# A reordered plan for windowed attention with a gated feed-forward: GpSimd's instructions beside VectorE's on PSUM

## The chip, the cores and the metric

The kernel runs on one core of one Trainium2 chip. The metric is device time in microseconds of one execution. TensorE (PE in the profile) multiplies matrices and writes to PSUM; VectorE (DVE), ScalarE (ACT) and GpSimd (POOL) do elementwise work; SyncE (SP) issues all transfers here. Each engine works through its own instructions in the order in which the program issues them, and waits at one whose inputs or output buffer are not ready.

## The reference

```python
batch, n_heads, seq, head_dim = (8, 8, 576, 64)
scores = scale * np.matmul(q, k.transpose(0, 1, 3, 2))
mask = (rel >= 0) & (rel < window)            # window = 64
scores = np.where(mask, scores, -1000000000.0)
scores = scores - np.max(scores, axis=-1, keepdims=True)
attn = np.exp(scores)
attn = attn / (np.sum(attn, axis=-1, keepdims=True) + 1e-09)
attn_out = np.matmul(attn, v)
...
x = attn_out.transpose(0, 2, 1, 3).reshape(B * S, H * D)     # 4608 tokens x 512
h = x @ w_in                                   # 512 x 2048
sp = np.maximum(h, 0.0) + np.log1p(np.exp(-np.abs(h)))
g = h * erf(sp)
return (g @ w_out).astype(np.float32)          # 2048 x 512
```

## The kernel before

The 4608 tokens are cut into 36 units of 128 tokens for the attention and 18 chunks of 256 tokens (two units) for the feed-forward. A chunk's feed-forward is done in two groups, one for each half of the 2048 hidden columns, so there are 36 groups `g`. Products are built from float16 pairs: each operand is split into a high part (a scaled copy, `scaled` or `narrow`) and a low part (what is left, `rest`), and three products are added.

The order of the whole program is written out by hand in one string, `PLAN`, of 2794 tokens. A token names a function and its arguments; where it ends in `v`, `a` or `g`, that letter puts the instruction on VectorE, ScalarE or GpSimd. The program issues the tokens one after the other, so the string fixes the order on every engine and in SP's queue of transfers. The steps are, with their tokens and lines:

- Loads of a unit: `lq`, `lk`, `lv` (L376 to L382). `pk` takes the largest magnitude of each (L392 on ScalarE, L394 on VectorE); `pa pb px py pc` turn the maxima into a chunk's scales.
- `qh kh vh` make the high parts (L366 ScalarE, L368 VectorE, L370 GpSimd) and `ql kl vl` the low parts (L373, VectorE).
- `s` is the score product (L449), `m` adds the mask and takes the row maximum from PSUM (L458, VectorE), `f` subtracts it (L463), `e` takes the exponential twice on ScalarE (L472, L473), `r` makes the low part (L477), `t` transposes by DMA (L480), `a` multiplies by the values (L487), `n` divides by the sum from PSUM (L492 to L494).
- `xh`, `xl` split the output (L504 or L502, L510) and `xt` transposes it by DMA. From group 8 on, the first feed-forward product is a seven-product (Strassen-like) one: `T` makes sums of `x` (L520, three steps with the index k), `yh` and `yl` split them (L504 or L502, L531; part 0 has 768 columns and part 1 has 512), `yt` transposes them.
- `M:g:m` is one of the seven products (L705). Products 1, 6, 7 and 4 pile up in one PSUM bank, and after each of them `E:g:k` copies the bank out (L502 on ScalarE, L504 on VectorE). Products 2, 5 and 3 pile up in the other, and `C:g:k` adds the bank to `h` (L720, VectorE). The next product into a bank waits for that reader. The first groups use `mm` and `ev` instead (L661).
- `sp` and `er` are softplus and erf on ScalarE (L726, L730), `gt` multiplies by `h` (L734, VectorE), `gh` and `gl` split the gated values (L366 or L368, L373), `mA` and `mB` are the second product with the high and with the low part (L753), `fo` scales or adds it into the output (L762, L368 or L366), `st` stores.
- `dc` and `gn` are one instruction each on a few scale columns (L646, L651).
- The weights are loaded by `L` and split at the start (`d c o b mb mx my mc h l dg lp le`); `U Uh Ul` make the weight sums of the seven products (L689, L502 or L504, L695).

ScalarE has one table of functions active at a time. Exponential, softplus and erf stand in different tables, and each change costs an `ACT_TABLE_LOAD`; the order of `e`, `sp` and `er` on ScalarE sets how many there are.

From about group 23 on the string repeats with a period of one chunk: two groups of feed-forward and two units of attention. The attention runs some chunks ahead of the feed-forward, so the last four groups have no attention beside them.

Of the kernel before, what the change touches and what calls it, by code (L numbers as in the profile page):

```python
# [19 lines left out]
W = 64  # L20
# [30 lines left out]
    "lq:0 lk:0 s:0 lm lq:1 m:0:1 f:0:1:g lk:1 lv:0 m:0:0 pk:0:2:v lv:1 e:0:1 f:0:0:g s:1 e:0:0 m:1:0 L:1 pk:1:2:v "  # L51
    "pa:0 r:0:1:g pb:0 f:1:0:v px:0 L:0 r:0:0:v L:3 py:0 pc:0 t:0:0 c:1 vh:1:a d:1 lq:2 c:0 m:1:1 o:1 lk:2 d:0 "
    "f:1:1:v o:0 vh:0:g s:2 d:3 t:0:1 e:1:0 c:3 b:0:a vl:0 a:0:0 b:1:a o:3 a:0:1 vl:1 L:2 mb:0 L:9 r:1:0:v d:2 e:1:1 "
    "c:2 L:8 lq:3 o:2 b:3:a mx:0 t:1:0 b:2:a m:2:0 my:0 c:9 mc:0 r:1:1:g m:2:1 L:11 dg:0 h:0:v d:9 n:0 f:2:0:g "
    "f:2:1:g lv:2 h:1:a c:8 lp:0:1 lp:1:0 t:1:1 o:9 lv:3 lk:3 xh:0:a mb:1 le:0:1:a d:8 lk:4 le:1:0:a d:11 lq:4 "
    "lp:0:0 pk:2:2:v mx:1 L:10 c:11 pk:3:2:v lp:1:1 s:3 my:1 o:8 e:2:0 xl:0:g L:4 e:2:1 a:1:0 L:5 a:1:1 b:9:a b:8:a "
    "o:11 m:3:0 pa:1 c:10 le:0:0:a pb:1 xt:0:0 mc:1 r:2:0:g n:1 xt:0:1 r:2:1:g m:3:1 h:2:a xh:1:a le:1:1:a px:1 mb:4 "
    "t:2:0 f:3:0:g pk:4:0:v dg:1 t:2:1 f:3:1:g py:1 lp:2:0 mx:4 pc:1 xl:1:v d:10 o:10 lp:2:1 vh:2:a my:4 dc:0:g vl:2 "
    "h:3:v b:11:a vh:3:v b:10:a a:2:0 a:2:1 e:3:1 lk:5 xt:1:1 mb:5 e:3:0 le:2:1:a xt:1:0 le:2:0:a mm:0:0 vl:3 "
    "ev:0:0:a mx:5 pk:4:1:a mc:4 my:5 lv:4 r:3:0:g l:3 dg:4 pk:4:2:v mc:5 lq:5 dg:5 n:2 c:4 L:6 xh:2:v t:3:0 h:9:a "  # L60
    "pk:5:1:a mm:0:1 h:10:v r:3:1:g d:4 mm:0:2 lv:5 o:4 h:11:a t:3:1 pk:5:0:a pk:5:2:v c:5 L:7 lp:9:1 ev:0:1:a a:3:1 "
    "pa:2 a:3:0 xl:2:g pb:2 xt:2:0 n:3 px:2 ev:0:2:v xh:3:a le:9:1:v lp:9:0 mm:0:3 b:4:a c:7 py:2 ev:0:3:a xt:2:1 "
# [12 lines left out]
    "t:4:1 h:12:g L:15 a:4:0 fo:1:1:a a:4:1 er:2:0 n:4 xh:4:v pk:9:1:a W:1 vh:6:a lp:12:1 ql:7 dc:6:g t:5:1 lp:12:0 "
    "d:15 t:5:0 mm:2:2 f:6:0:g a:5:1 vl:6 dc:7:v L:14 dc:4:v f:6:1:g c:15 ev:2:2:a le:12:1:a c:14 o:15 a:5:0 n:5 "
    "d:14 o:14 le:12:0:a mm:2:3 b:15:a mm:3:0 b:14:a lq:9 mb:7 vh:7:g s:7 vl:7 xh:5:a mx:7 my:7 xl:4:g ev:2:3:a "
    "ev:3:0:v mm:3:1 e:6:1 pk:9:0:a e:6:0 xl:5:v lv:9 xt:5:0 gt:2:0 lv:8 mc:7 V:1 m:7:0 h:15:v r:6:1:v dg:7 ev:3:1:v "
    "mm:3:2 xt:5:1 pk:8:2:v pk:9:2:v gh:2:0:a lp:15:0 lp:15:1 r:6:0:g le:15:0:v pa:4 sp:3:0 gl:2:0 mm:3:3 h:14:g "
    "xt:4:1 sp:2:1 m:7:1 f:7:0:g le:15:1:a pb:4 px:4 er:2:1 t:6:0 xt:4:0 mA:2:0:1 ev:3:2:a t:6:1 U:0:7:0:0:v er:3:0 "  # L80
    "py:4 a:6:1 a:6:0 l:14 f:7:1:v ev:3:3:a mA:2:0:0 U:0:7:1:0:v pc:4 gt:3:0 U:0:7:2:0:v sp:3:1 gt:2:1 gn:3:g mm:4:0 "
    "Uh:0:7:0:a mB:2:0:0 gh:2:1:a e:7:0 gh:3:0:a Ul:0:7:0:v kh:8:v kl:8 U:1:7:0:0:v gl:2:1 gn:2:g lk:10 vh:8:v "
    "mB:2:0:1 r:7:0:v ev:4:0:a e:7:1 mA:2:1:0 er:3:1 mm:4:1 U:1:7:1:0:g gl:3:0 kh:9:g t:7:0 mA:2:1:1 n:6 U:1:7:2:0:v "
    "ev:4:1:a r:7:1:v Uh:1:7:0:a mm:4:2 kl:9 t:7:1 qh:8:a gt:3:1 ql:8 Ul:1:7:0:v U:2:7:0:0:g xh:6:a mB:2:1:1 "
    "mB:2:1:0 s:8 a:7:0 fo:2:1:v a:7:1 m:8:1 sp:4:0 fo:2:0:v lk:11 lq:10 gn:5:v m:8:0 st:0:1 U:2:7:1:0:g mm:4:3 "
    "gh:3:1:a vh:9:a f:8:1:v n:7 mA:3:0:0 vl:9 gl:3:1 lv:11 mB:3:0:0 mA:3:1:0 er:4:0 xl:6:g qh:9:a ev:4:3:v gt:4:0 "
# [745 lines left out]
```

## Time and profile before

| what | value |
|---|---|
| median of three runs | 913.55 us (910.85 to 913.95) |
| profiled execution | 915.73 us, of which the span of instructions is 914.0 us |
| TensorE busy | 843.7 us, 92% |
| VectorE busy | 776.8 us, 85%, 1644 instructions |
| ScalarE busy | 696.7 us, 76% |
| GpSimd busy | 279.6 us, 31%, 230 instructions |
| granted TensorE clock, mean | 0.983 |

A line of a group names the source line, the engine, the operation, output and inputs by the program's names, shapes and count; then the busy time in us, the mean of one in ns, and the idle time of the engine just before these instructions with what ended it. A line of the timeline has the start in us, the duration in us, the engine, the line and the operation, and in square brackets the idle time before it with its releaser. A line of a stretch has its bounds, its length, and then the busy us of PE, weight loads (PEld), DVE, ACT and POOL with instruction counts, the granted clock, the busy share of the DMA engines and the GB/s that they moved.

### The profile page before, as it was taken

To read this page: it belongs to the slowest core of one execution; us is meant where nothing else is said; L and a number is where in the kernel's file an instruction comes from. 1 tells how busy PE (TensorE), PEld (TensorE's weight loads), DVE (VectorE), ACT (ScalarE), POOL (GpSimd) and SP (SyncE) were. 2 spreads that over 40 slices of the span, in tenths; PEclk is the share of its full clock that TensorE was granted. 3 is DMA by queue.
4 is the path that set the end of the run, shared out by engine and by line. 5 is a ranking of instruction groups with operands and counts; after the bars stand their busy time and mean duration, and the time that the engine had idled before them with its cause. 6 is when DMAs were issued, how large, how long until landed. Compare 5 with 4: busy or idle time off the path is not lost.

```text
span 914.0 us, 25226 instructions
## 1 busy us (share of the span) xinstructions
PE 843.7 (92%) x10726; PEld 583.9 (64%) x10726; DVE 776.8 (85%) x1644; ACT 696.7 (76%) x848; POOL 279.6 (31%) x230
## 2 busy tenths in 40 slices
PE   2579999998998999999998899999999999999998
PEld 2256556666676677667667567676767676766763
DVE  6789999999997998999796999999999997655453
ACT  5779889987997899877886678777777876644551
POOL 2431532422262564323234323232323232200000
PEclk9789999999998999999999999999999999999999
DMA  9992474364374744565363545455444432311000
GB/s 336 367 269 79 157 193 97 89 132 105 74 166 50 188 97 119 124 114 129 88 111 73 128 96 126 90 125 91 115 102 115 102 68 45 74 39 21 24 15 33
DMA packets 163489, 104.34 MB, mean 114 GB/s; under 512 B 140208, under 2 KB 140336, under 8 KB 163376
## 3 DMA queue, kind: packets, MB, share of 16 engines
q1 hardware_dynamic: 163376, 102.73, 47.0%
q8 instruction: 84, 1.38, 0.6%
q14 instruction: 29, 0.24, 0.1%
HBM read 59.44 MB, written 9.44 MB: 75 GB/s over the span
## 4 chain that ended last, share of the span: by engine, by line
DVE 38%; PE 36%; ACT 13%; issue 6%; DMA 5%; SPq 1%; POOL 1%; DVEq 0%; ACTq 0%; POOLq 0%
PE o L753 16%; PE hp L705 15%; DVE gl L373 5%; DVE sm L458 4%; DVE y L734 3%; DVE vs L373 2%; DVE h L720 2%; PE hp L661 2%; ACT y L726 2%; DVE qs L373 2%; DVE arena L531 2%; DVE gh L368 2%; ACT y L730 2%; ACT L730 2%; DVE peaks L394 2%
## 5 line engine op out<-in xcount | busy, mean ns | idle before, releaser
L753 PE MATMUL o<-w,gh 128*128 128x512 f16 x1152 | 269.2, 381 | 1.9 <-DVE ob L762 1.2
L753 PEld LDWEIGHTS <-gh 128*128 128x128 f16 x1152 | 109.2, 98 | 121.7 <-issue 5.9
L705 PE MATMUL hp<-arena,w 128*128 128x128 f16 x2688 | 168.9, 221 | 11.6 <-DVE h L504 10.1
L705 PEld LDWEIGHTS <-w 128*128 128x128 f16 x2688 | 158.9, 99 | 28.9 <-issue 14.5
L502 ACT ACTIVATE h<-hp 128x512 f32<-128x512 f32 x112 | 65.9, 589 | 113.3 <-PE hp L705 105.4
L753 PE MATMUL o<-w,gl 128*128 128x512 f16 x576 | 142.5, 379 | 1.3 <-DVE gl L373 1.1
L705 PEld LDWEIGHTS <-arena 128*128 128x128 f16 x2016 | 118.1, 98 | 18.3 <-issue 5.6
L705 PE MATMUL hp<-arena 128*128 128x128 f16 x2016 | 125.3, 220 | 4.6 <-ACT h L502 4.6
L373 DVE SCALAR_TENSOR_TENSOR gl<-y,sgh,gh 128x1024 f16<-128x1024 f32 x72 | 101.5, 1419 | 18.5 <-ACT gh L366 12.0
L734 DVE TENSOR_TENSOR y<-h,y 128x1024 f32<-128x1024 f32 x72 | 92.0, 1282 | 13.5 <-ACT y L730 13.5
L463 POOL TENSOR_TENSOR sm<-sm,mx 128x512 f32<-128x512 f32 x45 | 60.8, 1353 | 104.0 <-DVE mx L458 92.2
L661 PE MATMUL hp<-arena,w 128*128 128x256 f16 x768 | 87.6, 273 | 3.4 <-ACT h L502 2.0
L753 PEld LDWEIGHTS <-gl 128*128 128x128 f16 x576 | 52.5, 98 | 55.1 <-DVE gl L373 2.5
L720 DVE TENSOR_TENSOR h<-hp,h 128x512 f32<-128x512 f32 x84 | 57.3, 683 | 35.2 <-PE hp L705 35.2
L661 PEld LDWEIGHTS <-w 128*128 128x128 f16 x768 | 74.6, 98 | 17.5 <-issue 4.8
L726 ACT ACTIVATE y<-h,c 128x1024 f32<-128x1024 f32 x72 | 80.1, 1143 | 2.2 <-DVE gl L373 1.6
L477 POOL TENSOR_TENSOR p<-sm,p 128x512 f16<-128x512 f32 x33 | 44.8, 1357 | 119.8 <-ACT sm L473 117.1
L730 ACT ACTIVATE y<-y 128x1024 f32<-128x1024 f32 x72 | 75.3, 1053 | 0.5
L458 DVE CUSTOM_DVE_ANT_0 sm<-s,mask 128x128 f32<-128x128 f32 x288 | 65.3, 281 | 7.6 <-PE s L449 7.5
L366 ACT ACTIVATE gh<-y,sgh 128x1024 f16<-128x1024 f32 x45 | 51.3, 1140 | 23.0 <-DVE y L734 15.4
L726 ACT ACT_TABLE_LOAD x41 | 52.6, 1283 | 18.3 <-DVE h L720 17.6
L730 ACT ACT_TABLE_LOAD x46 | 59.0, 1283 | 0.8
(163 smaller groups left out, 1274.8 us busy)
## 6 DMA issues: line engine op xcount, KB each, us to landing
vr<-v_in SPq DMA_DIRECT2D x36, 512.0 KB, 4.1
kr<-k_in SPq DMA_DIRECT2D x36, 384.0 KB, 3.9
qr<-q_in SPq DMA_DIRECT2D x36, 256.0 KB, 3.9
out<-ob SPq DMA_DIRECT2D x34, 256.0 KB, 2.5
arena<-w_in SPq DMA_DIRECT2D x4, 1024.0 KB, 10.1
w<-w_in SPq DMA_DIRECT2D x4, 1024.0 KB, 7.0
arena<-w_out SPq DMA_DIRECT2D x4, 1024.0 KB, 5.5
w<-w_out SPq DMA_DIRECT2D x4, 512.0 KB, 9.2
```

The lines of the kernel that those rows point to most:

```text
L366: nc.scalar.activation(dst, src, AF.Copy, scale=s)
L373: nc.vector.scalar_tensor_tensor(dst, src, s, hi, op0=ALU.mult, op1=ALU.subtract)
L458: nc.vector.tensor_tensor_reduce(smi(u, par)[:, j, :], sps[par][:, j, :], mask[:, var, :], 1.0, LOWEST, op0=ALU.add, op1=ALU.max, accum_ou ...
L463: eng_of(eng).tensor_tensor(s, s, m.unsqueeze(2).broadcast_to([P, HP, P]), op=ALU.subtract)
L502: nc.scalar.activation(dst, src, AF.Copy)
L661: nc.tensor.matmul(hps[pc % 2][:, f, :], w1[a][:, cc, fs], xt[b][c % 2][:, cc:2 * NCC:NCC, :], start=(n == 0), stop=(n == 3 * NCC - 1))
L705: nc.tensor.matmul(bank[:, q, f, :], left(m, a, 2 * hf + q)[:, cc, f * P:(f + 1) * P], xt[b][c % 2][:, slot + cc, :], start=m in (1, 2, 5) ...
L720: nc.vector.tensor_tensor(dst, bank_view(1), dst, op=ALU.add)
L726: nc.scalar.activation(at(yb, g, n), at(hb, g, n), AF.Softplus, scale=st_c[g][:, n:n + 1])
L730: nc.scalar.activation(y, y, AF.Erf)
L734: nc.vector.tensor_tensor(y, at(hb, g, n), y, op=ALU.mult)
L753: nc.tensor.matmul(ops[j], a[:, f, ts], w2[b][:, hf * GF + f, :], start=f == 0 and a is gh and b == 0, stop=f == GF - 1 and a is gl)
```

## The change

Only `PLAN` changes. The same 2794 steps are issued in another order, and some with another engine letter. Counted over the whole string, these numbers of instructions change engines (net):

| step | VectorE | ScalarE | GpSimd |
|---|---|---|---|
| `yl` (768 columns / 512 columns) | -7 / -8 | | +7 / +8 |
| `vh` | +7 | | -7 |
| `T`, steps 0 / 1 / 2 | +7 / -3 / +6 | | -7 / +3 / -6 |
| `r` | +5 | | -5 |
| `kh` | | +6 | -6 |
| `E` | +5 | -5 | |
| `fo` | +4 | -4 | |
| `xh` | +4 | -4 | |
| `h` | -6 | +3 | +3 |
| `U`, `f`, `qh` | +3, +1, +2 | 0, 0, -1 | -3, -1, -1 |
| `gh` | -2 | +2 | |
| `dc` | -10 | | +10 |
| `gn` | -4 | | +4 |
| `pk` of q / of k | -6 / +6 | +6 / -6 | |

The order of ScalarE's steps gives 38 softplus, 44 erf and 32 exponential table changes, against 41, 46 and 38 before. The string again repeats with a period of one chunk in its second half. GpSimd has ten instructions in such a chunk, against eleven: before `T` (steps 2 and 0), `gn`, `f` three times, `kh`, `r` twice, `xl` and `vh`; after `T` (step 1), `f` twice, `xl`, `yl` twice, `r`, `dc` and `gn` twice.

At the start, the loads of the first weights and of the values come ahead of the first keys and queries. The diff, cut to the start and to one repeated chunk (from `M:26:1` on):

```diff
-    "lq:0 lk:0 s:0 lm lq:1 m:0:1 f:0:1:g lk:1 lv:0 m:0:0 pk:0:2:v lv:1 e:0:1 f:0:0:g s:1 e:0:0 m:1:0 L:1 pk:1:2:v "
...
-    "lv:33 r:30:0:g xt:28:1 mA:23:1:0 gl:24:0 t:30:0 gl:23:1 M:26:1 pk:32:1:a t:30:1 mB:23:1:1 E:26:0:a pk:33:0:v "
-    "C:25:2 M:26:6 pk:33:2:v yh:14:0:v E:26:1:a T:14:1:v s:31 pa:16 pb:16 fo:23:1:v T:14:2:g mB:23:1:0 gn:29:g px:16 "
-    "gh:24:1:v py:16 sp:25:0 M:26:2 pc:16 fo:23:0:v sp:25:1 qh:32:v mA:24:0:1 qh:33:a m:31:0 kh:32:v kl:32 M:26:7 "
-    "er:25:1 mA:24:0:0 C:26:0 f:31:0:g E:26:2:a gt:25:1 er:25:0 ql:32 M:26:5 kh:33:g m:31:1 M:26:4 ql:33 E:26:3:a "
-    "dc:28:v a:30:1 gl:24:1 a:30:0 s:32 n:30 f:31:1:g mB:24:0:0 gt:25:0 e:31:1 mB:24:0:1 M:27:1 C:26:1 kl:33 "
-    "gh:25:0:a vh:32:a M:26:3 yt:14:0:0 mA:24:1:1 C:26:2 e:31:0 gn:24:v r:31:1:v dc:33:v mA:24:1:0 E:27:0:v t:31:0 "
-    "r:31:0:g yh:14:1:v sp:26:0 st:11:1 m:32:1 M:27:6 lk:35 t:31:1 sp:26:1 vl:32 mB:24:1:1 st:11:0 yl:14:1:v M:27:2 "
-    "m:32:0 f:32:1:g er:26:0 mB:24:1:0 C:27:0 E:27:1:a yl:14:0:v a:31:1 xh:30:a a:31:0 lq:34 gl:25:0 yt:14:0:1 "
-    "M:27:7 e:32:1 lv:34 gh:25:1:v yt:14:1:1 M:27:5 E:27:2:v xl:30:g fo:24:1:v M:27:4 vh:33:g xt:30:0 fo:24:0:a "
-    "f:32:0:v mA:25:0:1 gt:26:0 E:27:3:a mA:25:0:0 r:32:1:v pk:34:0:a n:31 lk:34 pk:35:1:a er:26:1 mB:25:0:0 C:27:1 "
-    "T:15:0:g lq:35 mB:25:0:1 e:32:0 vl:33 pk:34:2:v mA:25:1:1 gt:26:1 gh:26:0:a yt:14:1:0 M:27:3 lv:35 r:32:0:g "
-    "xt:30:1 mA:25:1:0 gl:26:0 t:32:0 gl:25:1 M:28:1 pk:34:1:a t:32:1 mB:25:1:1 E:28:0:a pk:35:0:v C:27:2 M:28:6 "
...
+    "L:0 d:0 lv:1 pk:1:2:v c:0 o:0 lv:0 L:1 pk:0:2:v lk:0 pa:0 c:1 lq:0 pb:0 px:0 d:1 s:0 b:0:a lm o:1 lq:1 py:0 "
...
+    "pk:32:0:a t:30:0 M:26:1 r:30:1:v m:31:0 yt:13:0:1 lv:33 mA:23:1:0 E:26:0:a n:29 sp:25:0 M:26:6 T:14:0:v "
+    "mB:23:1:0 pk:33:2:v E:26:1:v T:14:1:g mA:23:1:1 pk:32:2:v C:26:0 pa:16 fo:23:0:v yh:14:0:v M:26:7 gh:24:0:v "
+    "yt:14:0:0 gl:24:0 mB:23:1:1 E:26:2:a st:11:0 pb:16 t:30:1 fo:23:1:v M:26:5 m:31:1 er:25:0 M:26:4 px:16 er:25:1 "
+    "C:26:1 f:31:1:g py:16 xl:28:g M:26:3 gt:25:1 mA:24:0:1 pc:16 gt:25:0 mA:24:0:0 qh:32:a E:26:3:a ql:32 f:31:0:v "
+    "M:27:1 gh:24:1:v e:31:1 mB:24:0:0 kh:32:v kl:32 mB:24:0:1 qh:33:a T:14:2:v gh:25:0:a C:26:2 xt:28:1 a:30:0 "
+    "gl:24:1 a:30:1 e:31:0 s:32 M:27:2 ql:33 E:27:0:a r:31:0:v M:27:6 kh:33:v r:31:1:v sp:26:1 dc:31:v t:31:1 "
+    "yh:14:1:v mA:24:1:1 C:27:0 yl:14:1:g sp:26:0 lk:34 st:11:1 E:27:1:a yt:14:1:1 kl:33 mA:24:1:0 vh:32:v gl:25:0 "
+    "er:26:0 t:31:0 mB:24:1:0 gh:25:1:a M:27:7 fo:24:0:v xt:28:0 m:32:0 mB:24:1:1 m:32:1 f:32:0:g mA:25:0:0 lq:35 "
+    "vl:32 e:32:0 mB:25:0:0 dc:32:g f:32:1:v yt:14:1:0 E:27:2:v gn:31:g M:27:5 e:32:1 r:32:0:g lq:34 M:27:4 gn:26:g "
+    "n:30 yl:14:0:g lk:35 lv:34 C:27:1 pk:34:1:v a:31:0 er:26:1 a:31:1 s:33 vh:33:v fo:24:1:a xh:30:a gl:25:1 M:27:3 "
+    "E:27:3:a mA:25:0:1 C:27:2 gt:26:0 mB:25:0:1 vl:33 pk:35:1:a M:28:2 sp:27:1 gt:26:1 pk:35:0:a pk:34:0:a t:32:0 "
...
```

377 rows, old and new, of the table PLAN are left out of this document.

## The prediction, on record before the result

> **What bounds the kernel now.** I read the page first, then the busy time by stretches: the start, the aperiodic middle, the repeated chunks, and one such chunk.
>
> ```profile
> span 914.0 us, 25226 instructions
> PE 843.7 (92%) x10726; PEld 583.9 (64%) x10726; DVE 776.8 (85%) x1644; ACT 696.7 (76%) x848; POOL 279.6 (31%) x230
> 0.00:75.00 75.00, 42.77 (x469) 27.01 (x470) 58.82 (x161) 53.27 (x77) 27.43 (x37) 0.86 1.01 308
> 75.00:477.00 402.00, 384.64 (x4912) 266.51 (x4911) 375.34 (x833) 351.62 (x441) 148.81 (x113) 0.99 0.51 117
> 477.00:753.00 276.00, 260.45 (x3717) 186.92 (x3716) 254.01 (x526) 212.10 (x248) 90.91 (x70) 0.99 0.47 103
> 660.95:706.97 46.02, 43.93 (x626) 31.36 (x626) 43.03 (x90) 35.82 (x42) 14.39 (x11) 1.00 0.47 110
> ```
>
> PE is busy for 843.7 of 914.0 us, so 70.3 us is all that any order can win: 32.2 in the first 75 us (DMA share 1.01), 17.4 in the middle, 15.6 in the repeated chunks, some 5 behind them. A chunk takes 46.02 us; PE is busy for 43.93 of it and DVE for 43.03. Both are nearly full, so I ask who waits for whom in that chunk, and look at the place in the timeline just ahead of 660.95.
>
> ```profile
> DVE gl L373 <- ACT gh L366: 2.0, 1, 2.0
> PE hp L705 <- DVE h L504: 1.7, 1, 1.7
> ...
> 656.31 1.37 POOL L510 TENSOR_TENSOR arena<-arena 128x512 f16<-128x512 f32 x1 [2.50 <-ACT arena L502]
> 656.59 2.18 DVE L373 SCALAR_TENSOR_TENSOR gl<-y,sgh,gh 128x1024 f16<-128x1024 f32 x1
> 657.67 2.09 POOL L370 TENSOR_SCALAR vs<-vr,csc 128x1024 f16<-128x1024 f32 x1
> 658.69 1.61 DVE L368 TENSOR_SCALAR gh<-y,sgh 128x1024 f16<-128x1024 f32 x1
> 660.22 0.67 DVE L504 COPY h<-hp 128x512 f32<-128x512 f32 x1
> 660.95 1.22 PE L705 MATMUL hp<-arena,w 128*128 128x128 f16 x19 [1.68 <-DVE h L504]
> ```
>
> Of PE's 2.09 idle us, 1.68 is one wait: the next product waits for the copy `E` (L504), and ahead of that copy stand `gl` with 2.18 us and `gh` with 1.61, both beside POOL. What these cost without POOL is seen at the end of the run (from 822 us on, POOL idle):
>
> ```profile
> L373 DVE SCALAR_TENSOR_TENSOR gl<-y,sgh,gh 128x1024 f16<-128x1024 f32 x10 | 12.6, 1278 | 6.0 <-PE o L753 4.9 <-ACT gh L366 1.1
> L720 DVE TENSOR_TENSOR h<-hp,h 128x512 f32<-128x512 f32 x10 | 6.9, 688 | 18.4 <-PE hp L705 18.4
> L368 DVE TENSOR_SCALAR gh<-y,sgh 128x1024 f16<-128x1024 f32 x5 | 3.7, 745 | 0.0
> L504 DVE CAST arena<-arena 128x512 f16<-128x512 f32 x1 | 0.4, 417 | 0.0
> ```
>
> So POOL lengthens `gl` by 0.90 us and `gh` by 0.87 there, together 1.77: the 1.68 us of PE. Reading PSUM costs DVE nothing: `C` (L720) takes 688 ns alone and 683 over the whole run.
>
> ```profile
> L720 DVE TENSOR_TENSOR h<-hp,h 128x512 f32<-128x512 f32 x84 | 57.3, 683 | 35.2 <-PE hp L705 35.2
> ```
>
> The Trainium skill, "SBUF — State Buffer", section "Who interferes with whom", gives the rule: GpSimd and VectorE share one port pair as a lock; a VectorE instruction with two SBUF inputs or in a two-port mode collides, one with at most one SBUF input outside those modes does not. The trace agrees as to who collides. By a full lock `gl` would lose what was left of the POOL instruction, 1.09 us, where the trace gives 0.90; with 1.09 the sum below would gain about 0.2 us a chunk, 1 us in all.
>
> **The change, part by part.** The rows of the one chunk on DVE:
>
> ```profile
> L373 DVE SCALAR_TENSOR_TENSOR gl<-y,sgh,gh 128x1024 f16<-128x1024 f32 x4 | 5.9, 1504 | 2.0 <-ACT gh L366 2.0
> L734 DVE TENSOR_TENSOR y<-h,y 128x1024 f32<-128x1024 f32 x4 | 5.0, 1239 | 0.0
> L458 DVE CUSTOM_DVE_ANT_0 sm<-s,mask 128x128 f32<-128x128 f32 x16 | 3.6, 279 | 0.0
> L373 DVE SCALAR_TENSOR_TENSOR vs<-vr,csc,vs 128x1024 f16<-128x1024 f32 x2 | 3.2, 1598 | 0.0
> L373 DVE SCALAR_TENSOR_TENSOR ks<-kr,csc,ks 128x768 f16<-128x768 f32 x2 | 2.7, 1342 | 0.0
> L368 DVE TENSOR_SCALAR gh<-y,sgh 128x1024 f16<-128x1024 f32 x2 | 2.3, 1174 | 0.0
> L531 DVE TENSOR_TENSOR arena<-arena 128x512 f16<-128x512 f32 x1 | 1.5, 1525 | 0.0
> L762 DVE SCALAR_TENSOR_TENSOR ob<-o,sg,ob 128x512 f32<-128x512 f32 x2 | 1.5, 738 | 0.0
> L477 DVE TENSOR_TENSOR p<-sm,p 128x512 f16<-128x512 f32 x2 | 1.4, 680 | 0.0
> L394 DVE TENSOR_REDUCE peaks<-vr 128x1 f32<-128x512 f32 x2 | 1.3, 674 | 0.0
> L646 DVE TENSOR_SCALAR c<-kw,cpw 128x2 f32<-128x2 f32 x2 | 1.2, 610 | 0.0
> L504 DVE CAST arena<-arena 128x512 f16<-128x512 f32 x1 | 1.0, 976 | 0.0
> L531 DVE TENSOR_TENSOR arena<-arena 128x768 f16<-128x768 f32 x1 | 0.9, 941 | 0.0
> L368 DVE TENSOR_SCALAR ks<-kr,csc 128x768 f16<-128x768 f32 x1 | 0.6, 615 | 0.0
> L504 DVE CAST arena<-arena 128x768 f16<-128x768 f32 x1 | 0.6, 552 | 0.0
> ...
> 692.12 1.01 DVE L373 SCALAR_TENSOR_TENSOR ks<-kr,csc,ks 128x768 f16<-128x768 f32 x1
> 804.42 1.34 PE hp L705 x24
> 805.76 1.73 PE o L753 x8
> ```
>
> *Contention in a repeated chunk.* Above the lone price: `gl` 4 x 0.226 = 0.90, `vl` 2 x 0.32 = 0.64 (same form as `gl`), `kl` 2 x 0.33 = 0.66 (against 1.01 at 692.12), `gh` 2 x 0.43 = 0.86, `yl` 0.845 (against the 680 ns of the same shape), the cast 0.56: 4.5 us of DVE.
>
> *Work moved in that chunk.* DVE gains `T` step 0 (0.68), one `r` (0.68), one `f` (0.68, same shape), one `kh` (0.615) and two `vh` (0.745 each, the form of `gh`): 4.1. It loses both `yl` (0.94 and, alone, 0.68), one `dc` (0.61) and one `qh` (some 0.5, by its size against `kh`): 2.7. One `gn` less and `pk` of k for q cancel within 0.3 (estimate). Net +1.4.
>
> *Contention that stays.* `f:31:1` follows `m` and runs beside `px` and `C:26:1`, `f:32:0` beside `m:32:1`, `r` beside `n`, `T` step 1 beside `pk`: none of these DVE instructions reads two SBUF tensors at length. But `xl:28` comes straight behind `f:31:1`, when DVE is at `gt:25:1`: up to 1.37 (its price at 656.31); I take 1.1, since `f` overlaps a little less than planned. `yl:14:1` outlasts `C:27:0` by 1.37 - 0.68 and meets `kl:33`: 0.6. `yl:14:0` has half as many columns again, about 2.1 (estimate); `C:27:1` and `pk:34:1` cover most: 0.3. The small `dc` and `gn` and the ends of `f`: 0.4. Sum 2.4; bounds 0 and the 4.5 of now or somewhat above. DVE's chunk comes to 43.0 - 4.5 + 1.4 + 2.4 = 42.3 us, 0.7 below now: not much, so it is the place that decides.
>
> *PE's wait.* Ahead of `E:26:1` on DVE there now stand `m`, `n`, `T` and `pk` in place of `gl` and `gh`, and PE has `mB` before product 6: the 1.68 us go. What is late next is `C:26:1`, for which product 3 waits. From the end of product 6 DVE has to do `E` 0.67, `pk` 0.67, `C` 0.68, `pa` 0.3 (estimate), `fo` 0.74, `yh` 0.55, `gh` 0.75, `gl` 1.28, `fo` 0.74, `m` 1.0 (four of 0.28, overlapped), `px` 0.4 (estimate), `C` 0.68: 8.5 us. PE in that time has two `mB` (0.87 each, half of the 1.73), one `mA` 1.73, three products of 1.34 and about 0.4 of `pb` and `py`: 7.9. That leaves a wait of 0.6. Elsewhere PE has slack: `M:27:2` comes some 2 us behind `C:26:2`. So a chunk wins 1.7 - 0.6 = 1.1, and the 276 us of repeated chunks, six of them, 6.5 us. Bounds: 12.5 won (all 2.09 each) and, where DVE keeps all contention, the loss under the rivals.
>
> *The middle.* Unrepeated order, DVE 375 of 402 us busy, POOL 17.0 us per 46 against 14.4 in the chunk: the same disease, but 17.4 us of idle PE are all that can go. I take 7; bounds 0 and 12. A step that serves both `E` and `fo` moves from ScalarE to DVE here (five and four instructions, 0.67 and 0.74 each): hidden only while DVE has room, which the removed contention gives.
>
> *Table loads.* Eleven fewer (114 against 125) at the price of this row, 14.1 us of ACT:
>
> ```profile
> L726 ACT ACT_TABLE_LOAD x41 | 52.6, 1283 | 18.3 <-DVE h L720 17.6
> 4.63 1.99 PE L449 MATMUL s<-kr,qr 64*64 64x128 f32 x32 [4.63 <-DMA kr<-k_in]
> ```
>
> ACT is busy for 35.8 of 46 us in a chunk, so most is covered by PE's and DVE's work: I count 1 us in the middle; bounds 0 and 3. Nine more splits on ACT (`kh` +6, `h` +3) use up most of what the loads free.
>
> *The start.* Two pieces of `w_in` and two units of values now go through SP's queue ahead of the first keys: by their shapes 3.1 MB, at the 308 GB/s of this stretch 10 us, and the first scores wait for keys (4.63 us now). The bytes needed before the first feed-forward product are nearly the same, and the weights' own chain starts earlier. I take +2; bounds -4 and +10.
>
> *SP and POOL as queues.* In a chunk `t:30:1` now stands behind `yt:14:0:0` and a store, and `t:31:0` behind `yt:14:1:1`, which waits for POOL's `yl:14:1`; `a:31` is a dozen PE steps later, so I cost it at nothing. If that cover went, `a` would wait for the rest of a POOL instruction, 1 to 2 us a chunk. The end without attention: 0.
>
> Sum: +2 - 7 - 6.5 - 1 = -12.5, so 903.2 against the profiled 915.73. The median of the runs is 2.2 below that execution, so 901.
>
> **The rivals.**
>
> *The waits only move (915).* The place ahead of `C:26:1` is 0.6 by my count, with 8.5 against 7.9; if `T`, `r` and `vh` make DVE late before product 6 too, the chunk gives the 1.7 back. For it: DVE has only 3.0 idle us a chunk and gets 1.4 of work. Against: 4.5 of contention.
>
> *DVE becomes the bound (slower, 927).* POOL's instructions start when their inputs come, not when DVE reads PSUM. If they still meet `gt`, `kl` and `gl`, DVE has 43.0 + 1.4 and its 3.0 of waits: 47.4, or +1.4 a chunk, +20 over the 678 us with attention; with half of that in the middle, +13. It decides once more than 4.5 - 1.4 = 3.1 us of contention stay. The same page of the Trainium skill says that whoever starts first holds the pair for the whole instruction; by that, a late POOL start ahead of `gt` costs all of it. For it: `xl` and `yl` have no PSUM work long enough beside them.
>
> *All of PE's waits go (886).* Chunks -12.5, middle -12, start -2, tables -1: 915.73 - 27.5, less 2.2. For it: nearly all slack in PE's new order is over 1 us. Against: the middle also waits for DMAs and tables.
>
> **How the numbers follow.** Forecast 0.50 (892 to 909), all waits gone 0.17, only moved 0.15, DVE bound 0.18. About 0.5% is what a measurement of this kernel tells from no change: 909 to 918. Faster 0.67, same 0.15, slower 0.18. The range reaches into both outer cases: 884 to 922; the likeliest case's own is 892 to 909.
>
> **What would show it.** `gh` (L368) near 750 ns and `gl` (L373) below 1400; `E`'s 1.7 us wait gone from a chunk, with a shorter one of `C` (L720); a chunk of 44.5 to 45.2 us; POOL's chunk below 14.39. Wrong: a chunk of 46 or more, `gt` (L734) well above 1239, or a first feed-forward product more than 5 us later.

## The result and the profile after

The changed kernel takes 890.89 us (median of four runs, 889.11 to 891.25) against 912.2 us (910.39 to 913.95): a ratio of 0.9763 with a 95% interval of 0.9735 to 0.979, 21.3 us faster. The forecast was 901 in a range of 884 to 922. The time lies in the range, 1 us below the likeliest case's own 892 to 909 and nearer to the rival of 886 than to 901. The direction was right; the gain is 21.3 us where 12.5 was forecast. The profiled execution took 891.25 us, its span 889.5.

From the page of after: the span, the engines, and the chain that ended last by engine.

```profile
span 889.5 us, 25238 instructions
PE 839.4 (94%) x10726; PEld 581.8 (65%) x10726; DVE 750.6 (84%) x1647; ACT 689.3 (77%) x840; POOL 248.1 (28%) x229
...
PE 62%; DVE 19%; DMA 7%; ACT 5%; issue 3%; POOL 2%; SPq 1%; DVEq 0%; POOLq 0%; ACTq 0%
```

The same chain of before:

```profile
DVE 38%; PE 36%; ACT 13%; issue 6%; DMA 5%; SPq 1%; POOL 1%; DVEq 0%; ACTq 0%; POOLq 0%
```

Read the chain first: before, the last instruction goes back through VectorE and ScalarE for half of the span, after through TensorE for 62% of it. The busy time by the same stretches as before, and one repeated chunk (columns as in the prediction):

```profile
0.00:75.00 75.00, 39.41 (x434) 23.43 (x434) 50.27 (x146) 49.57 (x69) 23.05 (x33) 0.89 1.00 292
75.00:477.00 402.00, 395.71 (x4999) 273.98 (x5000) 378.46 (x857) 360.08 (x454) 142.61 (x122) 0.99 0.54 124
477.00:753.00 276.00, 272.59 (x3981) 198.65 (x3979) 253.97 (x562) 214.27 (x249) 72.71 (x64) 1.00 0.50 102
663.62:708.08 44.46, 43.63 (x626) 31.33 (x626) 41.66 (x91) 36.24 (x43) 11.87 (x11) 1.00 0.53 111
```

Length less PE's busy time is PE's idle time. It went from 32.2 to 35.6 us in the first 75 us, from 17.4 to 6.3 in the middle, from 15.6 to 3.4 in the repeated chunks, and from 5.2 to 4.8 behind them: 20.2 us less in all. PE's busy time fell by another 4.3 (843.7 to 839.4). Together that is the 24.5 us between the spans.

The groups of VectorE that the prediction named, over the whole run:

```profile
L373 DVE SCALAR_TENSOR_TENSOR gl<-y,sgh,gh 128x1024 f16<-128x1024 f32 x72 | 93.4, 1299 | 4.4 <-ACT gh L366 2.7 <-PE o L753 1.2
L734 DVE TENSOR_TENSOR y<-h,y 128x1024 f32<-128x1024 f32 x72 | 89.5, 1254 | 4.2 <-ACT y L730 4.2
L368 DVE TENSOR_SCALAR gh<-y,sgh 128x1024 f16<-128x1024 f32 x25 | 20.4, 815 | 2.1 <-PE o L753 2.1
```

`gl` takes 1299 ns (1419 before, 1278 alone) and `gt` 1254 (1282 before); `gh` takes 815 (1021 before) where 745 is the price alone. A collision here is a VectorE instruction lengthened by a GpSimd instruction beside it. Summed over VectorE's instructions with a GpSimd one beside them, each by its time above the median of those of its line, tiles and form that have none, the collisions cost VectorE some 74 us before and 36 after (73.8 and 35.8, worked out from the two traces). What that bought in one chunk, from the waits of after in 663.62 to 708.08 (us in all, times, longest):

```profile
PE hp L705 <- DVE h L720: 0.4, 1, 0.4
...
PE av L412 <- DVE cdiag L409: 0.4, 1, 0.4
```

The 1.7 us wait for the copy `E` (L504) is gone. A wait of 0.44 for `C` (L720) is what came next, and the timeline of after shows where it is from:

```profile
661.92 1.04 POOL L463 TENSOR_TENSOR sm<-sm,mx 128x512 f32<-128x512 f32 x1 [7.48 <-DVE mx L458]
662.00 0.97 DVE L409 SCALAR_TENSOR_TENSOR cdiag<-ctop,ident 3x3 bf16<-3x3 f32 x1
662.90 0.67 DVE L720 TENSOR_TENSOR h<-hp,h 128x512 f32<-128x512 f32 x1
662.91 2.81 POOL L510 TENSOR_TENSOR arena<-arena 128x512 f16<-128x512 f32 x1
...
663.50 1.20 DVE L734 TENSOR_TENSOR y<-h,y 128x1024 f32<-128x1024 f32 x1
663.62 1.50 PE L705 MATMUL hp<-arena,w 128*128 128x128 f16 x24 [0.44 <-DVE h L720]
...
664.81 0.94 DVE L361 TENSOR_SCALAR csc<-cpw 128x3 int32<-128x3 int32 x1
...
675.69 1.16 POOL L531 TENSOR_TENSOR arena<-arena 128x512 f16<-128x512 f32 x1 [9.97 <-issue]
676.08 1.59 DVE L373 SCALAR_TENSOR_TENSOR ks<-kr,csc,ks 128x768 f16<-128x768 f32 x1
```

Directly ahead of `C` on VectorE stands `cdiag`, three by three elements, part of `px`: 0.97 us, because `f` runs on GpSimd beside it. That is the collision that is left on PE's path.

### The profile page after: what moved, and what is told of

Same layout as the page of the kernel before. It is cut to its first block, busy times and chain, and to the rows that moved or that the text cites. A ratio compares the mean times of both kernels' runs of the same rounds, so it can differ in the third digit from the quotient of the medians.

```text
span 889.5 us, 25238 instructions
## 1 busy us (share of the span) xinstructions
PE 839.4 (94%) x10726; PEld 581.8 (65%) x10726; DVE 750.6 (84%) x1647; ACT 689.3 (77%) x840; POOL 248.1 (28%) x229
## 4 chain that ended last, share of the span: by engine, by line
PE 62%; DVE 19%; DMA 7%; ACT 5%; issue 3%; POOL 2%; SPq 1%; DVEq 0%; POOLq 0%; ACTq 0%
PE o L753 30%; PE hp L705 22%; PE hp L661 3%; PE av L487 2%; PE s L449 2%; DVE gl L373 2%; DVE sm L458 2%; DMA pt<-p 2%; PE o L624 2%; DMA pt<-arena 1%; DMA arena<-w_out 1%; DVE y L734 1%; DMA kr<-k_in 1%; DMA qr<-q_in 1%; DVE misc L689 1%
## 5 line engine op out<-in xcount | busy, mean ns | idle before, releaser
L753 PE MATMUL o<-w,gh 128*128 128x512 f16 x1152 | 268.8, 379 | 2.0 <-DVE ob L762 0.9
L753 PEld LDWEIGHTS <-gh 128*128 128x128 f16 x1152 | 109.0, 98 | 119.7 <-issue 2.8
L705 PE MATMUL hp<-arena,w 128*128 128x128 f16 x2688 | 164.6, 219 | 3.2 <-DVE h L720 1.7
L705 PEld LDWEIGHTS <-w 128*128 128x128 f16 x2688 | 155.2, 98 | 17.1 <-issue 4.9
L753 PE MATMUL o<-w,gl 128*128 128x512 f16 x576 | 144.6, 379 | 0.0
L502 ACT ACTIVATE h<-hp 128x512 f32<-128x512 f32 x108 | 63.1, 587 | 71.2 <-PE hp L705 69.1
L373 DVE SCALAR_TENSOR_TENSOR gl<-y,sgh,gh 128x1024 f16<-128x1024 f32 x72 | 93.4, 1299 | 4.4 <-ACT gh L366 2.7
L734 DVE TENSOR_TENSOR y<-h,y 128x1024 f32<-128x1024 f32 x72 | 89.5, 1254 | 4.2 <-ACT y L730 4.2
L463 POOL TENSOR_TENSOR sm<-sm,mx 128x512 f32<-128x512 f32 x44 | 52.3, 1194 | 138.2 <-DVE mx L458 117.2
L753 PEld LDWEIGHTS <-gl 128*128 128x128 f16 x576 | 54.0, 98 | 55.3
L661 PEld LDWEIGHTS <-w 128*128 128x128 f16 x768 | 75.5, 99 | 15.6 <-issue 3.0
L720 DVE TENSOR_TENSOR h<-hp,h 128x512 f32<-128x512 f32 x84 | 57.5, 684 | 31.3 <-PE hp L705 28.7
L366 ACT ACTIVATE gh<-y,sgh 128x1024 f16<-128x1024 f32 x47 | 53.6, 1141 | 27.5 <-PE o L753 23.4
L473 ACT ACTIVATE sm<-sm,shift,cde 128x512 f32<-128x512 f32 x64 | 52.1, 814 | 2.1
```

Source lines behind the costliest of these rows:

```text
L366: nc.scalar.activation(dst, src, AF.Copy, scale=s)
L373: nc.vector.scalar_tensor_tensor(dst, src, s, hi, op0=ALU.mult, op1=ALU.subtract)
L463: eng_of(eng).tensor_tensor(s, s, m.unsqueeze(2).broadcast_to([P, HP, P]), op=ALU.subtract)
L502: nc.scalar.activation(dst, src, AF.Copy)
L661: nc.tensor.matmul(hps[pc % 2][:, f, :], w1[a][:, cc, fs], xt[b][c % 2][:, cc:2 * NCC:NCC, :], start=(n == 0), stop=(n == 3 * NCC - 1))
L705: nc.tensor.matmul(bank[:, q, f, :], left(m, a, 2 * hf + q)[:, cc, f * P:(f + 1) * P], xt[b][c % 2][:, slot + cc, :], start=m in (1, 2, 5) ...
```

## The experiments

The theory to test: VectorE's instructions that read two SBUF tensors or copy within SBUF were lengthened by GpSimd's, where PE waited for what stood behind them, and the change moved those instructions apart. The rivals: the order itself, ScalarE's tables, or work taken off an engine. Ratios are to the kernel before, run on the same chip. Kernels with added tokens have their lines a little lower: `T` at L522 and `gl` at L375, for instance. The end of a chunk is that of its last second product (L753) in the profiled execution.

**The order without the letters, and the letters without the order.**

```diff
 e1: the changed kernel's order; each step on the engine that it had before
-T:14:1:g  yl:14:1:g  vh:33:v ...
+T:14:1:v  yl:14:1:v  vh:33:g ...
 e2: the order of before; each step on the engine that it has after
```

> The changed order with every step on the engine it had before; the letters alone are undone. Theory A (the gain is that GpSimd's instructions stand where VectorE does not need the shared port, which takes order and letters together): the letters no longer fit their places, so the contention per repeated chunk is back near the 4.5 to 6 us of before and the time is 903 to 918. Theory B (the gain is the new order on TensorE, with more work between a product and the reader of its bank, and fewer table loads): the order keeps it, 890 to 898. TensorE's waits tell: by A the waits of L705 for VectorE's copies stand near the 9 us of before in the repeated stretch, by B under 3.

> The order of before with the engine letters of the changed kernel. Theory A: the 15 yl on GpSimd and the rest are not placed for this order, contention stays at 4 us a chunk or more, 908 to 922. Theory B: no new order, no gain, 910 to 925. A third theory, C (the gain is simply less GpSimd work, 248 against 280 us busy): most of the gain, 893 to 902.

Measured: 951.16 us for e1 (ratio 1.0436, 1.0414 to 1.0458) and 943.75 for e2 (1.0361, 1.0332 to 1.039). Nothing forecast that: each half alone loses more than the whole gains. Stretches of e1 (first), and of e2 (middle and a repeated chunk):

```profile
75.00:477.00 402.00, 358.99 (x4324) 245.42 (x4323) 347.38 (x764) 317.40 (x406) 135.50 (x101) 0.95 0.45 106
```

```profile
75.00:477.00 402.00, 357.58 (x4418) 246.24 (x4417) 354.89 (x769) 329.24 (x410) 139.15 (x108) 0.96 0.46 109
666.80:711.10 44.30, 43.76 (x626) 31.24 (x627) 41.71 (x90) 35.23 (x43) 13.52 (x10) 1.00 0.51 112
```

The loss is in the unrepeated middle: PE is busy for 359 and 358 of 402 us there, against 385 before and 396 after. In the repeated chunk the letters alone do what the whole change does, 44.3 us against 46.0, and the order alone does two thirds of it: 45.0 in e1 (718.7 to 763.7), with 5.5 us of collisions still in VectorE's chunk against 5.9 before, but a wait for `E` of 0.8 in place of 1.7. So the sum of the collisions does not decide there. Whether e1 gains by collisions at other places or by more work of PE ahead of the reader, which was theory B, is not separated. The repeated part is a question of its own. In the middle, order and letters seem to be a matched pair: DVE, ACT and PE are all less busy in e1 and e2, so they wait for each other. That is read from the busy times, and no run here tests it further.

**Two steps moved, nothing else.** The kernel before, with `xl` and `vh` of the repeated chunks on VectorE, so that POOL has nothing beside `gl` and `gh` ahead of `E`:

```diff
-xl:30:g  vh:33:g
+xl:30:v  vh:33:v
```

> The kernel before, with only ten steps of the last five chunks with attention changed: xl of units 26 to 34 and vh of units 27 to 35 go from GpSimd to VectorE, in their places (both behind the copy E:2 in VectorE's order). These are the two GpSimd instructions beside which gl took 2.18 us and gh 1.61. Theory A: gl and gh there fall to 1.28 and 0.75, TensorE's 1.68 us wait for E:2 goes, and a chunk falls from 46.0 to 44.3 to 45.3 us although VectorE does 1.4 us more work; about 4 chunks, so 907 to 911. Rival (VectorE's sum of work decides): the 1.4 us more are a longer chunk, 46.0 to 47.4, and 912 to 918.

Measured: 903.55 us (0.991, 0.9889 to 0.9932), 8.5 us below before, more than expected. Two repeated chunks of it, and PE's waits in 580 to 670:

```profile
580.60:625.00 44.40, 43.99 (x628) 31.40 (x627) 42.68 (x92) 35.88 (x43) 11.08 (x9) 1.00 0.55 111
625.00:669.30 44.30, 43.89 (x627) 31.29 (x627) 42.58 (x92) 35.78 (x43) 11.08 (x9) 1.00 0.51 113
```

```profile
PE av L404 <- DVE cmx L358: 0.5, 2, 0.2
PE hp L705 <- DVE h L720: 0.3, 2, 0.2
```

VectorE was given two more instructions a chunk (90 to 92) and is busy for less (43.03 to 42.6), and the wait for `E` is gone with 1.6 to 1.7 us of the chunk. That shows the mechanism: the collision, not the amount of work, held PE. It also gives as much in a repeated chunk as the whole change. The plan of e3 is that of before up to the end of chunk 9, and yet the profiled execution of before ends that chunk at 540.1 us and that of e3 at 535.5. So a difference of some 4 us between single executions says nothing in the middle; the medians and the repeated chunks do.

The same in the middle as well, from unit 8 on:

> The kernel before, with the local change (xl and the vh of GpSimd to VectorE) from unit 8 on instead of from unit 26: nine steps more, in the unrepeated middle. If the middle loses to contention in the same way as the repeated chunk: 898 to 902, against 903.6 with the change in the last chunks alone. If the middle is bound by VectorE's sum of work, the nine steps (some 6.6 us on VectorE) cost what they free: 903 to 907.

Measured: 906.37 us (0.9942, 0.9922 to 0.9962), so 3 us worse than e3 by the medians, on another chip; the intervals overlap. The repeated chunks stay at 44.4. From the end of chunk 4 to that of chunk 8, e11 takes 188.2 us, e3 184.4 and before 183.9. So in the middle the same move gains nothing and may cost some 4 us. That VectorE has no room for the nine steps there would explain it, but is not shown.

**No GpSimd at all** from group 8 on; all its steps go to VectorE in the changed order:

```diff
-dc:10:g  yl:4:0:g  f:12:1:g  kh:14:g  r:12:1:g ...
+dc:10:v  yl:4:0:v  f:12:1:v  kh:14:v  r:12:1:v ...
```

> The changed kernel with every GpSimd step from the first seven-product group on moved to VectorE in its place: no contention at all, but some 5.5 us more VectorE work in a repeated chunk (f twice, r, xl, both yl, T step 1, dc and gn), less the 2.5 us of contention left: 41.7 + 5.5 - 2.5 = 44.7 us of VectorE in a chunk with 43.6 of TensorE. Theory A: VectorE becomes the bound, a chunk of 45.3 to 47 us, 905 to 925 in all. Rival (what is left of contention costs more than GpSimd brings): 882 to 890.

Measured: 914.29 us (1.0024, 1.0004 to 1.0044). One repeated chunk:

```profile
684.50:729.50 45.00, 43.84 (x628) 31.46 (x627) 43.88 (x101) 36.27 (x44) 0.00 (x0) 1.00 0.53 110
```

With no collision left there, VectorE still has 43.9 of 45 us to do, and this chunk takes 0.5 us longer than in the changed kernel. Most of the loss lies elsewhere: chunk 8 ends at 493.3 us against 476.0, which is 17.3 of the 25.0 us between the two spans. GpSimd is worth 23 us of the time if it is placed well, and most of that in the middle.

**A doubled suspect, beside PSUM and beside SBUF.** Step 1 of `T` is issued four times instead of once in the last five chunks, in e6 at its place (beside `pk`, `E`, `C`, `fo`), in e9 behind `yl` (beside `kl`, `vh`, `gl`); in e5 part 1 of `yl` is issued three times:

```diff
 e6
-T:14:1:g
+T:14:1:g T:14:1:g T:14:1:g T:14:1:g
 e9
-yl:14:1:g
+yl:14:1:g T:14:1:g T:14:1:g T:14:1:g
 e5
-yl:14:1:g
+yl:14:1:g yl:14:1:g yl:14:1:g
```

> The changed kernel, with T step 1 of the last five chunks (GpSimd, 0.72 us) issued four times in a row instead of once: 2.2 us more GpSimd work a chunk, beside pk, E, C and fo, which read PSUM or one SBUF tensor. Theory A: VectorE loses under 0.5 us a chunk, the chunk stays at 44.4 to 44.7, 889 to 892 in all. Rival (the amount of GpSimd work matters): as much as the kernel with the doubled yl, 892 to 898.

> The changed kernel, with yl part 1 of the last five chunks (GpSimd, 1.16 us) issued three times in a row instead of once: 2.3 us more GpSimd work a chunk, beside kl, vh and gl, which read two SBUF tensors or copy within SBUF. Theory A: VectorE's instructions there grow by 1.5 to 2.3 us a chunk; a chunk goes from 44.5 to 45 to 46.5 us, as VectorE has 2.8 us of idle time a chunk and TensorE's slack at the next need is some 1.4; 892 to 898 in all. Rival (only the amount of GpSimd work matters, not its place): the same as the kernel with the doubled T.

> The changed kernel, with the same three extra T step 1 a chunk (GpSimd, 2.2 us, last five chunks) as in the earlier kernel with the doubled T, but issued behind yl part 1, where VectorE goes on to kl, vh and gl; no transfer waits for them, unlike the tripled yl. Theory A (place): VectorE's instructions there grow by 1 to 2 us a chunk where the earlier kernel's did not; the chunk goes from 44.5 to 45 to 46.5 and the whole to 893 to 898. Rival (the tripled yl cost its 4 us a chunk through the transposes behind it in SP's queue, not through the port): a chunk of 44.4 to 44.7, 889 to 892.

Measured: e6 890.92 us (0.9769, 0.9743 to 0.9796), e5 900.33 (0.9869, 0.984 to 0.9899), e9 891.23 (0.9784, 0.9752 to 0.9816). One chunk of e6, of e9 and of e5:

```profile
658.20:702.60 44.40, 43.64 (x627) 31.35 (x627) 41.58 (x91) 36.25 (x44) 14.07 (x13) 1.00 0.53 111
```

```profile
659.20:703.60 44.40, 43.58 (x627) 31.30 (x626) 42.54 (x91) 36.18 (x44) 15.84 (x13) 1.00 0.52 111
```

```profile
663.10:712.00 48.90, 45.51 (x627) 31.78 (x627) 45.31 (x91) 36.40 (x44) 16.41 (x12) 0.97 0.46 101
```

In e6 VectorE's busy time did not move (41.66 to 41.58) with three more GpSimd instructions. In e9 it rose by 0.9, as the timeline shows: `vh` (L370 here) and `gl` (L375) each lose some 0.47 us to the extra steps.

```profile
676.39 4.13 POOL L522 TENSOR_TENSOR arena<-arena 128x256 f32<-128x256 f32 x3
677.06 1.21 DVE L370 TENSOR_SCALAR vs<-vr,csc 128x1024 f16<-128x1024 f32 x1
678.19 1.75 DVE L375 SCALAR_TENSOR_TENSOR gl<-y,sgh,gh 128x1024 f16<-128x1024 f32 x1
```

Yet the chunk stayed at 44.4: at that place VectorE is ahead of PE by more than it loses. In e5 the tripled `yl` met more: VectorE lost 6.1 us of the chunk to collisions, against 2.3 in the changed kernel and 3.2 in e9, so e9 alone does not clear the collisions of e5's 4.4 us a chunk. Its waits in 612 to 760 say more (lines one lower there):

```profile
ACT L473 <- DMA pt<-p: 15.0, 3, 5.5
...
PE o L754 <- ACT ob L367: 7.6, 3, 3.0
```

`yt` waits for the tripled `yl` in SP's queue, the transposes `t` stand behind `yt`, so `p` is read late, the next exponential on ScalarE waits some 5 us until it may overwrite `p`, and the `fo` behind it holds PE: 2.6 of the 4.4 us in the chunk shown. PE's busy time there is 45.51 us against 43.63, at a granted clock of 0.97, and why is open. It is the queue that the prediction named under SP and POOL and costed at nothing, though there `a` was to be the one that waits. In the changed kernel PE has no such wait in these chunks.

**The collision on PE's path taken away.** In e8, the two `f` of an odd unit change engines and `xl` goes right behind step 1 of `T`, in the last five chunks:

```diff
+f:31:0:g            (right behind m:31:0)
-T:14:1:g
+T:14:1:g xl:28:g
...
-f:31:1:g py:16 xl:28:g
+f:31:1:v py:16
...
-f:31:0:v
```

> The changed kernel, last five chunks: f of the odd unit swaps engines between its halves, so that GpSimd's runs beside n instead of beside px, and xl comes right behind T step 1, beside E, pk, C and fo, instead of beside gt and the small scale steps. Theory A: the small instruction behind ctop (L409) falls from 0.97 us to 0.15, the one of csc (L361) from 0.94 to 0.17, xl from 2.81 to under 1.5; VectorE's chunk loses 1 to 1.6 us. TensorE is busy for 43.6 of 44.5 us, so the chunk gains 0.2 to 0.8 and the whole 1 to 3 us: 888 to 891. Rival (the new places collide with T and gh instead): no change or up to 2 us slower.

Measured: 887.93 us (0.9729, 0.9704 to 0.9754), 3 us below e6 on the same chip. One chunk and the place where after had its collisions:

```profile
659.20:702.90 43.70, 43.62 (x628) 31.40 (x627) 40.20 (x91) 36.29 (x44) 10.23 (x10) 1.00 0.54 113
```

```profile
653.94 1.16 POOL L510 TENSOR_TENSOR arena<-arena 128x512 f16<-128x512 f32 x1
...
661.53 0.15 DVE L409 SCALAR_TENSOR_TENSOR cdiag<-ctop,ident 3x3 bf16<-3x3 f32 x1
661.61 0.69 DVE L720 TENSOR_TENSOR h<-hp,h 128x512 f32<-128x512 f32 x1
...
664.14 0.17 DVE L361 TENSOR_SCALAR csc<-cpw 128x3 int32<-128x3 int32 x1
```

`cdiag` and `csc` take 0.15 and 0.17 us, `xl` 1.16 instead of 2.81, and PE idles for 0.08 of 43.70 us. In this chunk next to no wait of PE is left for an order to remove. This is the fastest of the kernels.

**The start.** The first query and key loads go to the head of the queue, ahead of the weights:

```diff
-L:0 d:0 lv:1 ... lk:0 pa:0 c:1 lq:0 pb:0 ...
+lq:0 lk:0 L:0 d:0 lv:1 ... pa:0 c:1 pb:0 ...
```

> The changed kernel with the first query and key loads put ahead of the first weight load in the queue, as before the change; nothing else. TensorE's busy time in the first 75 us fell from 42.8 to 39.4 with the change. If the late keys are the cause, the first scores start near 4.6 us again, 2 to 3.4 us come back and the time is 887 to 889; if the weights' chain or the transposes set the first feed-forward product, the time stays within 1 us of the changed kernel, or grows by up to 2.

Measured: 893.11 us (0.9797, 0.9773 to 0.9822), no gain. The first scores start at 13.6 us (12.8 in the changed kernel, 4.6 before), the first feed-forward product at 59.9 (58.7 and 56.6). PE's first row in e7, and the first scores of the changed kernel:

```profile
13.41 0.27 PE L404 MATMUL av<-ident,cmx 128*3 128x128 bf16 x1 [13.41 <-DVE cmx L358]
```

```profile
12.85 1.98 PE L449 MATMUL s<-kr,qr 64*64 64x128 f32 x32 [2.42 <-DMA qr<-q_in]
```

In both kernels PE's first instruction is that of `pb`, for which `pa` on VectorE has to finish, and the scores stand behind it. In the changed kernel `pb` comes at 10.16 us and the scores then wait 2.42 for the late queries. In e7 they do not wait for them, but `pb` comes only at 13.41, since the first weights and the values, behind which `pa` stands on VectorE, are loaded later. Late loads do hold the first scores; putting these two first only moves the wait.

**ScalarE's tables in the middle.** Five exponentials of one element, spread over groups 6 to 16 where ScalarE is between softplus and erf, put ten table loads back:

```diff
-gl:6:0 er:7:1
+gl:6:0 z er:7:1
+    (z: nc.scalar.activation, Exp, on one element)
```

> The changed kernel with five one-element exponentials put between two softplus or two erf steps of groups 6 to 16, to bring back ten table loads (12.8 us of ScalarE) in the middle. If table loads are hidden as the prediction's term of 1 us had it: 890 to 893. If ScalarE's order sets the middle: 896 to 904.

Measured: 903.87 us (0.9916, 0.9894 to 0.9939), 12.6 us above e9 on the same chip, for ten loads of 1.283, 12.8 us, and the five exponentials of 0.29 each, 1.5 us. Chunk 8 ends at 486.6 us (476.0 in the changed kernel, 474.5 to 476.8 in e5 to e9, which share its plan there); behind it the chunks are the same to 0.1 us. So here ScalarE's time has a price of most of its length, 12.6 of 14.3 us by the medians and 10.6 in the profiled execution, though ScalarE is busy for only 360 of 402 us.

**Collisions in the middle.** Two extra `T` steps behind `yl` in seven chunks of the middle:

```diff
-yl:7:1:g
+yl:7:1:g T:7:1:g T:7:1:g
```

> The changed kernel with two extra copies of T step 1 on GpSimd right behind the first part of yl in seven chunks of the unrepeated middle (u = 5 to 11): some 14 instructions of about 1 us, where VectorE then reads two SBUF tensors. It asks whether collisions have a price in the middle, as added table loads had. Theory A (the middle's order has no slack on VectorE either: what a collision takes from VectorE there goes into the time): VectorE's instructions in those chunks grow by 5 to 10 us in all and the time goes up by most of that, to 895 to 901. Theory B (the middle is set by ScalarE and by the sum of the work, and a collision is absorbed as in the repeated chunk): 889 to 893, with the same chunk ends as the changed kernel's within 2 us. If POOL's own queue is what gets late (r or f behind the extra steps), waits of TensorE for transposed p or for ScalarE's e appear instead.

Measured: 895.38 us (0.9827, 0.9805 to 0.9849; runs from 890.41 to 897.23, the profiled one being the shortest). VectorE lost 4.6 us more to collisions than in the changed kernel (40.3 against 35.8). The median is 4.5 higher, on another chip, as theory A had it. The profiled execution has these collisions and is no longer than the changed kernel: from the end of chunk 1 to the end of chunk 9 it takes 391.2 us, against 388.6 there, but 388.7 to 391.8 in e5 to e9, which have the same instructions in that stretch. So the trace shows no price, and the medians suggest one of up to the whole length; what a collision costs in the middle stays open.

## Why the prediction was right, point by point

*Contention in a repeated chunk: right, and shown* (e3, e6, e8). The signs that the forecast named were there: `gh` 815 ns (towards 750), `gl` 1299 (below 1400), the 1.7 us wait for `E` gone with a shorter one for `C` in its place, POOL's chunk 11.87 (below 14.39). The chunk, 44.46 us, is a little under the 44.5 to 45.2.

*What stays of it.* I forecast 2.4 us of collisions; by the same reckoning as above it is 2.3 in this chunk, but in other places, so that the agreement is luck. `gt` was to lose 1.1 to `xl` and lost nothing (1.20), while `xl` lost 1.65 (2.81 against 1.16 in e8) off the path; `kl` lost 0.58 (1.59 against 1.01), forecast 0.6; the small instructions, costed at 0.4 with the ends of `f`, lost 1.59 (`cdiag` 0.82, `csc` 0.77). VectorE's chunk came to 41.66, forecast 42.3, and that too by errors that cancel: 5.9 us of collisions were there before and not 4.5 (I left out `dc`, 0.61 us where 0.22 is the price alone, and a small step of L358), and by that VectorE's other work grew by some 2.3 and not 1.4.

*PE's wait.* The forecast was 0.6 us at `C:26:1`, and the wait there is 0.44. The place was right and the size luck: the count of 8.5 against 7.9 has no collision in it, and in e8, where `cdiag` keeps its 0.15 us, no wait is left there. The term of the sum was too small: 1.1 a chunk forecast, 1.56 measured. PE's idle time in it went from 2.09 to 0.83, and its busy time from 43.93 to 43.63. Over 477 to 753 us the term was 6.5, and PE's idle time fell by 12.2. These are its longest waits there before:

```profile
PE hp L705 <- DVE h L504: 9.0, 6, 1.7
PE hp L705 <- ACT h L502: 4.1, 3, 1.9
```

The first is gone after, and the waits behind `px` that replace it (`C` and `cdiag`) come to 2.5 us in all. The second, for copies `E` on ScalarE between 490 and 520 us, fell to 0.4; it was in no term of mine.

*PE's busy time* was not a term of my sum. It fell by 4.3 us. One group fell by as much with the same count, and no other by more than 0.4; before and after:

```profile
L705 PE MATMUL hp<-arena,w 128*128 128x128 f16 x2688 | 168.9, 221 | 11.6 <-DVE h L504 10.1 <-DVE h L720 1.3 <-DMA arena<-arena 0.3
```

```profile
L705 PE MATMUL hp<-arena,w 128*128 128x128 f16 x2688 | 164.6, 219 | 3.2 <-DVE h L720 1.7 <-DMA arena<-arena 1.5
```

The group is the one whose waits went, 11.6 to 3.2 us, and `E` (L504) is out of the list. Why its busy time falls with them is open: the granted clock rose only from 0.983 to 0.988, and the ends of these products are modelled.

*The middle: the mechanism was one of at least two, and the size was too small.* I took 7 us within bounds of 0 and 12; PE's idle time there fell by 11.1. Some 2 us of that may be chance, for in e3, with the instructions of before, it is 15.4 and not 17.4. The longest of PE's waits in 75 to 477, before and then after:

```profile
PE av L404 <- DVE cmx L358: 2.7, 3, 1.0
PE av L412 <- DVE cdiag L409: 2.3, 3, 1.3
PE hp L661 <- ACT h L502: 2.0, 1, 2.0
```

```profile
PE hp L705 <- DMA arena<-arena: 1.5, 1, 1.5
PE s L449 <- DVE mx L458: 1.2, 2, 0.6
```

Added up over all rows of that list, PE waited for VectorE 10.4 us before and 3.7 after, for ScalarE 4.9 and 0.4, for transfers 1.7 and 2.2. So PE waited some 6.7 us less for VectorE and 4.5 less for ScalarE. The first fits the collisions, whose price there e12 leaves open; the second fits the table loads. Neither is shown.

*The tables: a step that failed, in the count and most likely in the price.* I counted eleven loads fewer, worth 1 us within 0 to 3. The trace of after has 120 loads, of before 126 (46, 41, 38 and 1 in the first four rows):

```profile
L730 ACT ACT_TABLE_LOAD x44 | 56.5, 1283 | 0.7
L726 ACT ACT_TABLE_LOAD x41 | 52.6, 1283 | 8.9 <-DVE h L720 8.1
L472 ACT ACT_TABLE_LOAD x31 | 39.8, 1283 | 7.9 <-DMA pt<-p 6.7 <-DVE p L477 0.7
L392 ACT ACT_TABLE_LOAD x3 | 3.8, 1283 | 0.1
L568 ACT ACT_TABLE_LOAD x1 | 1.3, 1283 | 0.7 <-PEq L824 0.7
```

I had counted changes between softplus, erf and exponential alone; `pk` (L392) and a step of the weights (L568) load a table too, and then the next softplus does. The price was wrong the other way: "ACT is busy for 35.8 of 46 us in a chunk, so most is covered" was read from the repeated chunk and applied to the middle, where e10 pays for most of their length. In 75 to 477 us there are 60 loads before and 55 after, so the tables are worth 6.4 us of the 11.1 at the very most, their whole length. e10's price, somewhat lower, is of loads added to the changed kernel, and no run takes loads from the one before. How the middle's gain divides between tables, collisions and order is open: e12 fixes no price, and e1 and e2 show that the parts do not add.

*The start: right in size, half right in reason.* The first feed-forward product came 2.1 us later, forecast 2; PE's idle time in the stretch rose by 3.4. I let the first scores wait for keys behind the weights in SP's queue. They wait for queries there, but behind 10.2 us of waiting for `pa`, and with both loads first (e7) neither the scores nor the product are earlier.

*Behind the attention* I counted 0, and PE's idle time there changed by 0.4.

*The rivals.* That the waits only move (915) is out: the next wait is 0.44 where 1.68 was. That VectorE becomes the bound (927) did not happen; its +13 would be 14.5 by its own terms, 1.4 us in each of six chunks and half of that over the middle. Its rule can be seen at work. The Trainium skill, "SBUF — State Buffer", section "Who interferes with whom", has whoever issues first hold the shared pair for the whole instruction. In the timeline of after `csc`, three columns wide, ends at 665.75 with `xl` at 665.72, and `cdiag` with `f`: the trace agrees that VectorE waits out the rest of a GpSimd instruction. It does not agree on who is first by the recorded starts: `xl` starts 0.59 us ahead of the first `gt` and loses, and `gt` is untouched. Had the lock gone by those starts, `gt` would have lost about 0.6 us (1.16 less 0.59). That all of PE's waits go (886) is nearer to what happened than the forecast, though I gave it 0.17 against 0.50: the repeated chunks won 12.2 of its 12.5 us and the middle 11.1 of its 12, and the start lost 3.4 where it had 2 won. The 4.3 us less of PE's busy time were in no case.

## What to carry to other kernels

Look for what stands ahead of the instruction that the bottleneck engine waits for, and ask of that place alone what runs beside it: two steps moved there in each of five chunks (e3) gave 8.5 us, and collisions at a place with slack (e9) cost nothing. Before a cost is called covered, read the slack of the stretch where it lies: the table loads, called covered from the idle time of ScalarE in the repeated chunk, cost most of their length when added to the middle (e10). An order and the choice of engines that were made together should be tried together and by places, for half of such a change can lose 3.6 or 4.4% (e1, e2) where the whole gains 2.4%.

## What the runs showed of the hardware that was not expected

- The shortest instructions of VectorE pay most for their length beside GpSimd: `cdiag` (3x3) 0.97 us against 0.15, `csc` (128x3) 0.94 against 0.17.
- A GpSimd instruction can lose more than VectorE does: `xl` took 2.81 us where it met `gt`, 1.16 where it did not, and `gt` 1.20 in the first case and 1.22 in the second.
- Three of the 44 steps on ScalarE that take a largest magnitude (L392) have a table load of 1.283 us ahead of them, each directly behind a softplus, and the next softplus has one again.
